# An earlier verdict, one piece for two chunks of y, and smaller clears, in a one-core gated-attention and feed-forward kernel

## The chip, the cores and the metric

The kernel runs on one core of a Trainium2 chip. The core has five engines that run side by side, each through its own queue in program order: TensorE (PE; its weight loads are listed as PEld), VectorE (DVE), ScalarE (ACT), GpSimd (POOL) and SyncE (SP), which issues most transfers. The metric is the device time of one execution in microseconds (us). A time is the median of several executions.

## The reference

Inputs are q, k, v, a_re and a_im of shape 4 batches x 8 heads x 768 steps x 48, and four weight matrices. Everything is float32 in the reference.

```
mag   = sqrt(a_re**2 + a_im**2);  scale = minimum(mag, 0.999) / (mag + 1e-6)
a     = (a_re + i a_im) * scale                # per step and per key element d
S[t]  = a[t, :, None] * S[t-1] + outer(k[t], v[t])       # complex 48 x 48 state per head
y[t]  = q[t] @ real(S[t])
x     = y as 3072 tokens x 384                 # the heads side by side
out   = ((x @ w1) * (x @ w2)) @ w3 @ w_out     # 384 -> 1024 -> 1024 -> 384
```

## The kernel before

The four batches are cut into eight units u = 0 to 7 of half a sequence each (384 steps, all 8 heads); u even begins a batch, u odd goes on from the state that the even one left. A unit has three chunks c of 128 steps.

**Stages.** At the head the weights are read, converted, and w3 @ w_out is formed once as `w3o` (lines 1025 to 1074: `row_load`, `row_work`, `fuse`). For each unit `gates(u)` turns the gates into running products of magnitude and sums of angle with logarithms, exponentials, scans and sines on ACT and DVE, multiplies them into q and k, and moves the results into the layouts `QL` and `KL`. The attention of a unit is made of four steps: `turn` (line 724) transposes k on TensorE (`tp`) and copies it out as `KT` (ACT, L733); `state` (line 787) forms the chunk's contribution `kv` to the state and adds it into one of three buffers `T`; `scores` (line 736) forms q k for half the heads (`sc`, L745) and evicts the lower triangle into one of two buffers `A` with a predicated copy on DVE (L748); `outputs` (line 760) forms y of one chunk out of A and V, and of QL and T (L779), and copies it to `xT` (ACT, L781). The feed-forward part of unit u-1 runs among the attention of unit u: eight `ab` steps (L820 twice three products, an ACT copy, a DVE multiply L826), then the sums `So` (L848), one row block with `w3o` (L909, `o`), and for the other two row blocks seven half-size products `p1` to `p7` (L873) whose sums are formed on DVE (L855). Beside all this, from 101.9 us on, POOL runs `check_weights` (line 972): it reads parts of the inputs again and counts which elements lie in the range that the fast path needs (`look`, `seen`).

**The order.** `pieces(u)` lists the attention of a unit as a list of short lists; `unit` puts between them the feed-forward steps of the unit before (`rest`), evenly by count, except that the last two of `rest` come at the end. `run` emits them in this order on TensorE, and books the gate steps, the looks and other work of ACT, DVE, POOL and SP with a clock of its own (line 1171 on) wherever they fit. So a change in `pieces` also moves some instructions of ACT and DVE. Every engine executes its own queue strictly in order.

**The verdict.** `judge(0)` compares the extremes that were collected from the gates, and `seen`, with their limits (seven small DVE instructions, L1090 and L1092), and `judge(1)` sums the counts over the partitions with one TensorE product (L1097) and writes the verdict `good` (L1101). At the very end every engine loads `good` (L1356) and branches on it (L1357): if it is 0, the whole computation is done again by `general`, for any inputs; otherwise the engines jump past that code to the closing barrier (L1391).

**Padding.** Heads are 48 wide and stand 64 apart in V and T. TensorE reads windows of 32 columns that reach into the 16 columns of padding, so these must be zero.

Of the kernel before, what the change touches and what calls it, by code (L numbers as in the profile page):

```python
# [375 lines left out]
def kernel(  # L376
# [36 lines left out]
    nc = tc.nc  # L413
    B, H, D, S = qt.shape
# [102 lines left out]
    def take_qk(u):  # L517
        g = g_t.setdefault(u, {})
        g["q"] = gate_pool[u % 2].tile([P, KD, TT], FP, tag="q", name="q")
        g["k"] = gate_pool[u % 2].tile([P, KD, TT + 1], FP, tag="k", name="k")  # L520
# [196 lines left out]
    def step(ops, n=1):  # L717

        for _ in range(n):
            for op in ops:  # L720
                if op is None or op == "move":
                    break

    def turn(u, c, x):

        src = L_t[u][2 + x]
        if x == 0:
            KT_t[u, c] = two.tile([P, H, DG, 2, KD], FP, tag="KT", name="KT")
        tp = ps_v.tile([P, KD, C], FP, tag="v", name="tp")
        for f in range(KD):  # L730
            nc.tensor.transpose(out=tp[:, f], in_=src[:, f, c * C:(c + 1) * C], identity=ident)  # L731
        with tc.high_priority():
            nc.scalar.copy(out=KT_t[u, c][:, :, :, x].rearrange("p h d f -> p f d h"),  # L733
                           in_=tp.rearrange("p f (d h) -> p f d h", h=H))

    def scores(u, c, x):
        QL, KL = L_t[u][0:2]
        w = slice(c * C, (c + 1) * C)
        A = Ab[(u * UC + c) % 2]
        n = H // 2  # L740
        sc = Sc[x]
        for s0 in SPANS:
            for j in range(n):
                g = (s0 // SB + j) % LANES
                nc.tensor.matmul(out=sc[SB * g:SB * g + SB, j, s0:C], lhsT=KL[:, x * n + j, w][:, s0:s0 + SB],  # L745
                                 rhs=QL[:, x * n + j, w][:, s0:C], start=True, stop=True)
        with tc.high_priority():
            masked[:] = [nc.vector.copy_predicated(out=A[:, x * n:(x + 1) * n], data=sc,  # L748
                                      mask=mask)]
# [32 lines left out]

    Tb = [singles.tile([2 * D, H, 64], FP, name=f"T{i}") for i in range(3)]
    for T in Tb:
        nc.gpsimd.memset(T, 0.0)

    def state(u, c):

        KT, V = KT_t.pop((u, c)), g_t[u]["vr"][:, c].rearrange("p (h d) -> p h d", d=D)
        n = u % 2 * UC + c  # L790
        T = T_t.get((u // 2, n))
        kv = ps_v.tile([2 * D, H, D], FP, tag="v", name="kv")
        for hd in range(H):
            rows = KT[:, hd].rearrange("p d x f -> p (d x f)")
            for g in range(0, 2 * D, SB):
                nc.tensor.matmul(out=kv[g:g + SB, hd], lhsT=rows[:, g:g + SB], rhs=V[:, hd], start=True, stop=True)  # L796
        Tn = Tb[(u * UC + c) % 3]
        with tc.high_priority():
            if T is None:
                nc.scalar.copy(out=Tn[:, :, 0:D], in_=kv)  # L800
            else:
                add = nc.vector.tensor_tensor(out=Tn[:, :, 0:D], in0=kv, in1=T[:, :, 0:D], op=OP.add)
                if (u, c) == (0, 1):

                    tc.add_manual_dep(add.ins, begun[-1].ins.name, ORDER, reason="begun")
        if c == UC - 1:
            rho = L_t[u][1][:, :, TT:TT + 1].to_broadcast([2 * D, H, D])
            nc.vector.tensor_tensor(out=Tn[:, :, 0:D], in0=Tn[:, :, 0:D], in1=rho, op=OP.mult)
        T_t[u // 2, n + 1] = Tn
        if u + 1 < NU and c == UC - 1 - u % 2:  # L810
            load_v(u + 1)
# [211 lines left out]
    def rounding():  # L1023

        stack = ExitStack()
        for n, k in (("raw", 2), ("low", 2)):
            cv[n] = stack.enter_context(tc.tile_pool(name=n, bufs=k))
        return stack
# [74 lines left out]
    for A in Ab:  # L1103
        nc.vector.memset(A, 0.0)
    for V in Vb:
        nc.gpsimd.memset(V, 0.0)

    def pieces(u):

        sc = [[("sc", lambda c=c, x=x: scores(u, c, x)) for x in range(2)] for c in range(UC)]  # L1110
        tr = [[("tr", lambda c=c, x=x: turn(u, c, x)) for x in range(2)] for c in range(UC)]
        kv = [("kv0" if u % 2 == c == 0 else "kv" if c < UC - 1 else "rho", lambda c=c: state(u, c)) for c in range(UC)]
        y = [("y" if u % 2 or c else "y0", lambda c=c: outputs(u, c)) for c in range(UC)]

        if u % 2:
            return [[("need", u), tr[0][0]], [tr[0][1]], [tr[1][0], kv[0]], [tr[1][1]], [kv[1]], sc[0], sc[1] + [y[0]],
                    sc[2] + [y[1]], [y[2], ("end", u)]]
        return [[("need", u), tr[0][0]], [tr[0][1]], [tr[1][0], kv[0]], [tr[1][1]], [tr[2][0], kv[1]], [tr[2][1]],
                [kv[2]] + sc[0], sc[1] + [y[0]], sc[2] + [y[1]], [y[2], ("end", u)]]

    def ffn(u, parts=1):
        ab = [("ab", lambda j=j: ffn_ab(u, j)) for j in range(KF)]
# [8 lines left out]
    def unit(u, rest, ahead):  # L1131

        seq = [("begin", u)] + rest[:ahead]
        rest = rest[ahead:]
        p = pieces(u) + [[]]
        n = len(p)
        first = [i * (len(rest) - 2) // (n - 1) for i in range(n)] + [len(rest)] if u > 1 else [0, 1, 2, 3, 3, 4, 4, 5, 5, 5, 6]
        for i in range(n):
            seq += rest[first[i]:first[i + 1]] + p[i]
        return seq  # L1140
# [137 lines left out]
    with tc.manual_schedule(engines={mybir.EngineType.PE}):  # L1278

        phase = rounding()  # L1280
        row_load(0, 4)
        load_gates(0)
        row_load(1, 2)
        row_load(2)
        row_load(3)
        take_qk(0)
        steps = gates(0, True)
        for f in range(KF):
            row_work(f)
            if f == 0:  # L1290
                load_qkv(0)
            if f + 4 < KF:
                row_load(f + 4)
            if f == VLOAD:
                load_v(0)
                turn_v(0)
            if f >= KF - 2:
                continue
            for j in range(KF):
                fuse(f, j)  # L1300
            step(steps, (3, 2, 2, 2, 1, 1)[f])
        work = w12_work()
        for _ in steps:
            pass
        for f in work[:2]:
            f()
        for f in range(KF - 2, KF):
            for j in range(KF // 2):
                fuse(f, j)
        fill = [lambda f=f, j=j: [fuse(f, j + x) for x in range(2)] for f in range(KF - 2, KF) for j in range(KF // 2, KF, 2)]  # L1310
        steps = gates(1, False)
        take_qk(1)
        rest = ffn(0, 2)
        work = work[2:]
        for i, p in enumerate(pieces(0)):
            for kind, f in p:
                if kind not in ("need", "end"):
                    f()
            if i in (1, 3, 6, 9):
                fill.pop(0)()  # L1320
            if i == 0:
                for f in work[:2]:
                    f()
                load_qkv(1)
                turn_v(1)
            step(steps, 5 if i == 0 else i >= 6)
            if i in (5, 7):
                work[2 + (i == 7)]()
        with tc.manual_schedule(engines={mybir.EngineType.Activation, mybir.EngineType.DVE, mybir.EngineType.Pool, mybir.EngineType.SP}):

            paced.append(True)
            work[4](False)

            def head(i):
                rest[i][1]()
                if i in (2, 3):
                    work[2 + i]()
                if i == 4:
                    phase.close()
                    late.append(fast.enter_context(tc.tile_pool(name="late", bufs=1)))  # L1340
                    late.append(fast.enter_context(tc.tile_pool(name="looks", bufs=1)))
                    looks.append(check_weights(late[1]))
                    streams.append((1, out_weights()))
            seq = [("abw" if i in (2, 3) else "ab", lambda i=i: head(i)) for i in range(HEAD)]
            for u in range(1, NU):
                seq += unit(u, rest[HEAD:] if u == 1 else ffn(u - 1), AHEAD[u])
            seq += ffn(NU - 1, 2)
            gate["ops"] = steps
            clock.update(POOL=0.0, SP=0.0, DMA=0.0)
            ready.clear()  # L1350
            ready.update(at=6.5, r2=6.3, k=7.7)
            advance()
            run(seq[:-6] + [("judge", 0)] + seq[-6:-2] + [("judge", 1)] + seq[-2:])
    fast.close()

    value = nc.values_load(good[0:1, 0:1], min_val=0, max_val=1)  # L1356
# [38 lines left out]
```

## Time and profile before

| | before |
|---|---|
| median of 3 executions | 562.1 us (561.05 to 562.63) |
| the profiled execution, its own time | 560.6 us |
| its span in the trace | 558.7 us |
| granted TensorE clock, mean | 0.985 |
| TensorE busy | 524.4 us, 94% |
| VectorE busy | 364.0 us, 65% |
| ScalarE busy | 274.8 us, 49% |
| GpSimd busy | 362.7 us, 65% |
| share of TensorE in the chain that ended last | 79% |

Times inside the trace are microseconds from the start of the span. The chain of work that ended last is followed back from the last instruction to whatever released it; an engine's busy time says little where it runs beside others. In tables of instructions a name ending in q (POOLq, SPq) is an engine's sequencer: it runs loads of registers, branches, semaphores and DRAINs, which are not counted as busy. Products in float32 appear as two matmul instructions each, so x8 in the chain stands for four products.

### The profile page before, as it was taken

Reading aid. Unit: us, or ns where it says so; the run is one execution under the profiler, and the core shown is the slowest. Engines: PE = TensorE matmul, PEld = TensorE weight load, DVE = VectorE, ACT = ScalarE, POOL = GpSimd, SP = SyncE. Lnnn points to the kernel's source line nnn. Section 1 sums busy time; section 2 is a strip of 40 time slices with the busy share of each in tenths; the row PEclk is TensorE's granted clock in tenths of the full one; section 3 lists DMA queues with packets and bytes.
Section 4 is the critical chain, followed back from the end, with each engine's and each line's share of the span. In section 5 each row is a group of like instructions: output and inputs, shape, how many; then the busy total and the mean of one; then the engine's idle time right before and its main releaser. Section 6 shows DMA issues by size and latency. Waiting matters only on the chain.

```text
span 558.7 us, 13227 instructions
## 1 busy us (share of the span) xinstructions
PE 524.4 (94%) x5474; PEld 358.8 (64%) x5474; DVE 364.0 (65%) x514; ACT 274.8 (49%) x389; POOL 362.7 (65%) x425
## 2 busy tenths in 40 slices
PE   4779889998999999999999999999999999999993
PEld 2345565566656785669666875687567856696572
DVE  7998399778685866687576756695848664421141
ACT  6988766585377325742475237722774242111100
POOL 3000000198888888888899889898998888886000
PEclk9899979999999999999999999999999999999998
DMA  8996978279559626892579245943595228322001
GB/s 260 354 406 166 285 210 279 65 167 196 137 125 242 182 106 174 204 265 77 145 192 222 83 118 152 241 130 102 136 234 156 64 69 212 77 70 70 0 2 49
DMA packets 73190, 89.73 MB, mean 161 GB/s; under 512 B 31776, under 2 KB 62944, under 8 KB 72352
## 3 DMA queue, kind: packets, MB, share of 16 engines
q1 hardware_dynamic: 67040, 69.78, 47.2%
q0 software_dynamic: 6080, 19.01, 11.6%
q8 instruction: 45, 0.74, 0.6%
q14 instruction: 25, 0.20, 0.1%
HBM read 65.14 MB, written 4.72 MB: 125 GB/s over the span
## 4 chain that ended last, share of the span: by engine, by line
PE 79%; DVE 8%; ACT 5%; issue 2%; DMA 2%; SPq 1%; DVEq 0%; ACTq 0%
PE m L820 45%; PE p L873 11%; PE y L779 7%; PE o L909 6%; PE sc L745 5%; DVE So L848 2%; PE kv L796 2%; DVE gA L624 2%; PE tp L731 2%; PE f L1070 1%; ACT gZ L576 1%; ACT low L955 1%; DMA im<-in_a_im_dram 1%; DMA k<-in_k_dram 1%; ACT gR L576 1%
## 5 line engine op out<-in xcount | busy, mean ns | idle before, releaser
L820 PE MATMUL m<-xT,w1s 128*128 128x384 f32 x384 | 135.0, 488 | 0.0
L820 PE MATMUL m<-xT,w2s 128*128 128x384 f32 x384 | 134.3, 486 | 0.0
L820 PEld LDWEIGHTS m<-xT,w2s 128*128 128x128 f32 x384 | 73.0, 190 | 50.9
L820 PEld LDWEIGHTS m<-xT,w1s 128*128 128x128 f32 x384 | 71.4, 190 | 44.9
L826 DVE TENSOR_TENSOR ab<-m,a 128x384 f32<-128x384 f32 x64 | 35.4, 553 | 91.4 <-PE m L820 83.1
L1016 POOL TENSOR_SCALAR look<-look 128x256 f32<-128x256 f32 (+1 forms) x84 | 88.4, 1053 | 7.3
L997 POOL TENSOR_TENSOR seen<-seen,look 128x256 bf16<-128x256 bf16 (+1 forms) x84 | 69.5, 828 | 6.8
L825 ACT COPY a<-m 128x384 f32<-128x384 f32 x64 | 30.3, 473 | 77.8 <-PE m L820 77.8
L981 POOL MEMSET seen<- 128x256 bf16 x1 | 0.3, 312 | 101.9 <-DVE w2s L965 101.9
L1013 POOL TENSOR_TENSOR look<-look 128x256 f32<-128x256 f32 (+1 forms) x72 | 59.5, 826 | 1.9
L909 PE MATMUL o<-w3o,ab 128*128 128x384 f32 x160 | 54.1, 487 | 0.0
L1015 POOL TENSOR_SCALAR look<-look 128x256 f32<-128x256 f32 (+1 forms) x44 | 50.4, 1146 | 5.1 <-DMA look<-in_a_re_dram 1.9
L781 ACT COPY xT<-y 128x384 f32<-128x384 f32 x24 | 11.4, 477 | 76.6 <-PE y L779 76.6
L992 POOL DMA_DIRECT2D look<-in_w_dram x56 | 33.6, 599 | 16.6 <-POOL seen L997 16.6
L733 ACT COPY KT<-tp 128x384 f32<-128x384 f32 x40 | 34.0, 856 | 18.1 <-PE tp L731 17.9
L1018 POOL TENSOR_TENSOR look<-look 128x256 f32<-128x256 f32 (+1 forms) x44 | 39.4, 896 | 3.7
L748 DVE COPY_PREDICATED A<-mask,sc 128x512 f32<-128x512 uint8 x48 | 33.0, 732 | 13.3 <-PE sc L745 12.8
L909 PEld LDWEIGHTS o<-w3o,ab 128*128 128x128 f32 x160 | 29.5, 190 | 18.3 <-issue 0.2
L779 PE MATMUL y<-A,V 128*32 128x128 f32 x768 | 40.2, 278 | 0.0
L1070 PE MATMUL f<-wo_s,w3s 128*128 128x384 f32 x96 | 37.2, 534 | 1.6 <-issue 1.6
L745 PE MATMUL sc<-QL,KL 96*32 96x32 f32 (+3 forms) x1536 | 33.5, 239 | 4.1 <-DVE A L748 1.9
L745 PEld LDWEIGHTS sc<-QL,KL 96*32 96x32 f32 x1536 | 29.2, 112 | 10.6 <-DVE A L748 4.4
(121 smaller groups left out, 904.7 us busy)
## 6 DMA issues: line engine op xcount, KB each, us to landing
look<-in_w_dram POOLq DMA_DIRECT2D x56, 256.0 KB, 3.5
raw<-in_w_dram SPq DMA_DIRECT2D x6, 1024.0 KB, 10.2
raw<-in_w_dram SPq DMA_DIRECT2D x8, 768.0 KB, 8.9
KL<-gR SPq DMA_DIRECT2D x24, 192.5 KB, 5.0
KL<-k SPq DMA_DIRECT2D x24, 192.5 KB, 5.6
re<-in_a_re_dram SPq DMA_DIRECT2D x24, 192.0 KB, 3.4
im<-in_a_im_dram SPq DMA_DIRECT2D x24, 192.0 KB, 3.3
k<-in_k_dram SPq DMA_DIRECT2D x24, 192.0 KB, 8.8
```

The costliest lines, as they stand in the source:

```text
L745: nc.tensor.matmul(out=sc[SB * g:SB * g + SB, j, s0:C], lhsT=KL[:, x * n + j, w][:, s0:s0 + SB], rhs=QL[:, x * n + j, w][:, s0:C], start=T ...
L779: nc.tensor.matmul(out=o, lhsT=a, rhs=b, start=s0, stop=s1)
L820: nc.tensor.matmul(out=m, lhsT=w[:, j * P // WB, f, j * P % WB:j * P % WB + P], rhs=xT_t[u][:, f], start=(f == 0), stop=(f == KD - 1))
L826: nc.vector.tensor_tensor(out=ab_t[u][:, j], in0=got[1], in1=a, op=OP.mult)
L873: nc.tensor.matmul(out=m[p], lhsT=a[:, f], rhs=b[:, f], start=(f == 0), stop=(f == KH - 1))
L909: nc.tensor.matmul(out=m, lhsT=ab_t[u][:, f, t * P:(t + 1) * P], rhs=w3o[:, f], start=(f == 0), stop=(f == KF - 1))
L997: nc.gpsimd.tensor_tensor(out=seen[:, 0:n], in0=seen[:, 0:n], in1=x, op=OP.add)
L1013: tt(out=x, in0=x, in1=x, op=OP.mult)
L1015: ts(out=y, in0=x, scalar1=high, scalar2=None, op0=OP.is_le)
L1016: ts(out=x, in0=x, scalar1=low, scalar2=None, op0=OP.is_ge)
L1018: tt(out=x, in0=x, in1=y, op=OP.mult)
L1070: nc.tensor.matmul(out=sums[j], lhsT=w3_t[f][:, j * P:(j + 1) * P], rhs=w3_t["wo"][:, f], start=(f == 0), stop=(f == KF - 1))
```

## The change

Three edits are made.

1. `judge(0)` is emitted twelve pieces from the end of the sequence instead of six, and `judge(1)` ten from the end instead of two. The end of the sequence is the feed-forward part of unit 7: eight `ab`, `spart`, and p1, p2, p4, p6, p7, o, p5, p3. So `judge(0)` moves from before p4 to before `ab` 5, and `judge(1)` from before p5 to before `ab` 7.
2. The y of chunks 1 and 2 stand in one piece, so a unit has one piece less, and the feed-forward steps are spread over one gap less. The lists for units 0 and 1 are adapted.
3. The clears of V and T touch only the columns 48 to 63 of each head.

In the emitted queues nothing changes on TensorE in units 0 and 1. In units 2, 4 and 6 p6 and p7 now stand together ahead of the third pair of scores, and the last two y follow each other. In units 3, 5 and 7 the last two y follow each other too, p6 and p7 stand together ahead of the third pair of scores, and the `o` product stands ahead of the last transpose of k, with p1 between that transpose and `kv`. On VectorE the sums of p7 come ahead of the third pair of evictions, and in units 3 and 5 the multiply of q (L636) comes ahead of the first pair. On ACT, in units 3 and 5, the copy `KT` comes behind the copy `ot` (L913) and the first of the two functions on `gR` comes behind the copy `U` (L878). On SP the load of `good` stands ahead of the last five output transfers. V's first transfer and T's first writes no longer wait for POOL.

```diff
@@ state buffers @@
     for T in Tb:
-        nc.gpsimd.memset(T, 0.0)
+        nc.gpsimd.memset(T[:, :, D:64], 0.0)
@@ value buffers @@
     for V in Vb:
-        nc.gpsimd.memset(V, 0.0)
+        nc.gpsimd.memset(V.rearrange("p c h e -> p (c h) e")[:, :, D:64], 0.0)
@@ pieces @@
         if u % 2:
             return [[("need", u), tr[0][0]], [tr[0][1]], [tr[1][0], kv[0]], [tr[1][1]], [kv[1]], sc[0], sc[1] + [y[0]],
-                    sc[2] + [y[1]], [y[2], ("end", u)]]
+                    sc[2] + [y[1], y[2], ("end", u)]]
         return [[("need", u), tr[0][0]], [tr[0][1]], [tr[1][0], kv[0]], [tr[1][1]], [tr[2][0], kv[1]], [tr[2][1]],
-                [kv[2]] + sc[0], sc[1] + [y[0]], sc[2] + [y[1]], [y[2], ("end", u)]]
+                [kv[2]] + sc[0], sc[1] + [y[0]], sc[2] + [y[1], y[2], ("end", u)]]
@@ unit @@
-        first = [i * (len(rest) - 2) // (n - 1) for i in range(n)] + [len(rest)] if u > 1 else [0, 1, 2, 3, 3, 4, 4, 5, 5, 5, 6]
+        first = [i * (len(rest) - 2) // (n - 1) for i in range(n)] + [len(rest)] if u > 1 else [0, 1, 2, 3, 3, 4, 4, 5, 5, 6]
@@ unit 0 @@
-            if i in (1, 3, 6, 9):
+            if i in (1, 3, 6, 8):
                 fill.pop(0)()
...
-            step(steps, 5 if i == 0 else i >= 6)
+            step(steps, 5 if i == 0 else (i >= 6) + (i == 8))
@@ the sequence @@
-            run(seq[:-6] + [("judge", 0)] + seq[-6:-2] + [("judge", 1)] + seq[-2:])
+            run(seq[:-12] + [("judge", 0)] + seq[-12:-10] + [("judge", 1)] + seq[-10:])
```

## The prediction

> **What bounds the kernel now.** First I read the page: its chain of work that ended last is 79% TensorE, and TensorE is busy 94% of the span. So an edit counts if it shortens TensorE's own queue, fills one of its gaps, or shortens the two ends of the span where TensorE is not at work.
>
> ```profile
> PE 79%; DVE 8%; ACT 5%; issue 2%; DMA 2%; SPq 1%; DVEq 0%; ACTq 0%
> ```
>
> Second, the end. TensorE's last product ends at 549.9 and VectorE's last sum at 550.3, but the span is 558.7, and no engine is busy in those last 8 us. The instructions of `good` (start times are the last column), of line 1357 (the branch and what follows it), and of line 1391 (the closing barrier) fill them:
>
> ```profile
> L1356 POOLq TENSOR_LOAD <-good x1: 502/502/502, 547.5 to 547.5; - x1
> ...
> L1357 SPq EVENT_SEMAPHORE  x8: 17/17/17, 553.9 to 554.5; - x8
> ...
> L1357 POOLq COMPARE_BRANCH  x1: 45/45/45, 548.1 to 548.1; - x1
> ...
> L1357 SPq COMPARE_BRANCH  x1: 45/45/45, 551.0 to 551.0; - x1
> ...
> L1357 POOLq EVENT_SEMAPHORE  x1: 17/17/17, 550.8 to 550.8; - x1
> ...
> L1391 POOLq EVENT_SEMAPHORE  x4: 17/17/17, 557.9 to 558.6; - x4
> L1391 POOLq DRAIN  x3: 40/107/6933, 550.9 to 558.4; - x3
> L1391 SPq DRAIN  x3: 7/7/13, 555.3 to 558.1; - x3
> ```
>
> To be seen: POOL, idle since its last look ended at 513.9, gets the verdict at 547.5, branches at 548.1, does its next instruction at 550.8, and then spends 6.93 us in a DRAIN from 550.9 to 557.85. Its barrier instruction follows at 557.9. SP, the last of the others (it issues the last output transfer), signs the barrier at 555.3. So POOL ends the kernel, 2.5 us behind SP, and POOL's time is set by `good` (written at 547.4 to 547.5) and by nothing else that the trace shows.
>
> Third, the chain in order of time over unit 2, an even unit; columns are start, length, what:
>
> ```profile
> 195.44 1.25 PE sc L745 x64
> 196.69 0.88 PE y L779 x32
> 197.56 1.50 PE p L873 x8
> 199.06 1.25 PE sc L745 x64
> 200.32 1.76 PE y L779 x64
> 202.07 1.50 PE p L873 x8
> 203.57 1.90 PE y L779 x64
> 205.47 2.80 PE p L873 x16
> ```
>
> TensorE runs here without a gap, so its order matters only by what each kind costs behind another: a product p costs 1.50 us alone behind y or sc, but two in a row 2.80; a y costs 1.76 behind sc and 1.90 behind p. Fourth, the timeline of VectorE and POOL at the head:
>
> ```profile
> 4.19 1.79 DVE L961 TENSOR_SCALAR w3s<-raw 128x256 int32<-128x256 int32 x1
> ...
> 8.98 0.29 DVE L961 TENSOR_SCALAR w3s<-raw 128x256 int32<-128x256 int32 x1 [0.64 <-DMA raw<-in_w_dram]
> ...
> 11.56 0.56 DVE L591 TENSOR_TENSOR im<-im,gR 128x384 f32<-128x384 f32 x1 [0.38 <-DMA im<-in_a_im_dram]
> ...
> 3.14 2.69 POOL L1106 MEMSET V<- 128x1536 f32 x2
> ```
>
> The same 128x256 operation takes 1.79 us while POOL clears V, and 0.29 us afterwards.
>
> **The verdict.** `judge(0)` goes from before product 4 to before `ab` 5 of the last unit, `judge(1)` from before product 5 to before `ab` 7. No instruction is added. VectorE's part (six tests with their accumulator reads and one compare) ran from 538.58 to 540.51, 1.9 us. Behind the `ab` multiply at 523.84 to 524.40 it runs to about 526.4; the next multiply is due at 527.7, since VectorE waits 3.31 us for TensorE between two of them: nothing on the path. Its first instruction waits for POOL's last look; that ended at 513.92, 10 us sooner. The count product on TensorE (0.12 us on the chain, 547.00 to 547.12) costs 0.12 us in either place, and finds its operand ready. VectorE writes `good` right behind multiply 6 (531.58 plus 0.56): about 532.5 instead of 547.5. SP's load of the verdict now stands ahead of the last five output transfers, but these start near 544 and lose nothing.
>
> POOL then branches at 533.1, is past it at 535.9 (the 2.7 us of the rows), and its DRAIN ends at 542.8 if it stays 6.93 us. Next late is SP: last transfer issued until 550.99, branch at 551.04, next instruction 553.93 (2.85 us), 20 semaphore instructions until 555.33. ACT signs at 550.7, PE at 552.3, VectorE at 553.8, all from work that does not move. So the barrier closes at 555.38 instead of 557.90: **2.5 us**. What the trace does not show is why this DRAIN takes 6.93 us. Bounds: 2.5 us gained if it is POOL's own (it may grow to 19 us before it matters), nothing if it waits for something at the end of the kernel. I take 2.5: the instruction names no semaphore, POOL's own transfers had all ended at 510, and nothing else ends at 557.85.
>
> The Trainium skill (VectorE: DVE Perf Modes, "The DRAIN you can't avoid") gives the closing DRAINs of all engines as about 12 ns, always the same. The rows of ACT, PE, VectorE and SP agree (7 to 17 ns), POOL's 6.93 us does not; taken strictly, the rule would make those 6.9 us a hidden wait for the rest of the kernel and this term 0.
>
> **y of two chunks in one piece.** The same TensorE instructions in another order, in units 2 to 7. An even unit now runs y0, p6 p7, sc, y1 y2, p5 p3. Before, by the rows from y0 on: 1.50 + 1.25 + 1.76 + 1.50 + 1.90 + 2.80 = 10.71. After: 2.80 + 1.25 + 1.76 + 1.76 + 2.80 = 10.37. Gain 0.34, three times: 1.02. In an odd unit (chain from 241.22) the o product also moves ahead of the last transpose, and p1 between that and kv. Before: 0.33 + 5.16 + 0.81 + 1.50 + 1.26 + 1.50 + 1.25 + 1.76 + 1.50 + 1.25 + 1.76 + 2.80 + 1.90 + 2.80 = 25.58. After: 5.16 + 0.33 + 1.30 (p behind a transpose, as at 189.47) + 0.88 (kv behind p, as at 191.72) + 1.50 + 1.25 + 1.50 + 1.25 + 1.76 + 2.80 + 1.25 + 1.76 + 1.76 + 2.80 = 25.30. Gain 0.28, three times: 0.84. Together 1.86.
>
> Covers, unit by unit. (a) y2 now follows y1 at once and needs the third pair of score evictions on VectorE. In unit 2 the last product before the scores ends at 200.36, its two sums at 201.1, the pair (1.37 us) at about 202.5, and y1 at 203.37: 0.85 us in hand. (b) In odd units kv waits for ACT's copy KT, which now has only p1 beside it: transpose done at 246.87 by the row's lag, copy of 0.88 us from 246.95 to 247.83, kv due at 248.0: 0.2 us in hand, against 5.16 us before. (c) In units 3 and 5 the multiply q (L636, 1.43 us) now stands ahead of the first evictions on VectorE: it runs 250.9 to 252.3, the pair to 253.6, and the second score group wants those banks at 253.1 and 253.8: 0 to 0.2 us each. Its load of q landed at 249.5, 1.4 us sooner (unit 5: 367.0 against 369.5). The gaps before kv at 190.8, 309.5 and 428.5 (0.94, 1.22, 0.81 us) come from VectorE's sums and scans ahead of ACT's KT, which do not move; they stay. Bounds for this edit: 2.1 gained (nothing waits, and transitions cost a little less than the rows), 0.6 lost (covers (b) and (c) miss by 0.5 us each, in five places); I take 1.7, the sum less 0.15 for (c), since every cover computes as holding.
>
> **The clearing.** POOL's five memsets took 1.44 + 2.69 = 4.13 us. By their rows (0.48 us for 512 elements, 1.35 for 1536: 0.85 ns an element) the strided ones of 128 and 384 take 3 x 0.16 + 2 x 0.37 = 1.2 us, 4.1 us at most if strides cost as much as full rows. POOL has nothing else until 101.9, so only VectorE's 1.79 us operation can gain: up to 1.5. But VectorE then waits longer for the raw weights at 8.98 and for the transfer of im at 11.56, which nothing here makes earlier: 0. If it is wrong, up to 1.5 gained, or 0.5 lost when weight loads that SP can issue 0.6 us sooner slow the landing of im.
>
> The Trainium skill (SBUF — State Buffer, "Who interferes with whom") says that GpSimd and some VectorE forms exclude each other for a whole instruction; the 1.79 against 0.29 fits, and by the rule alone the head would gain the full 1.5 and the time come to 556.4.
>
> **Sum.** 2.5 + 1.7 + 0 = 4.2 us: the profiled execution's 560.6 (span 558.7 and 1.9 around it) would be 556.4. The median of the runs shown, 562.1, is 1.5 above that execution; taken off it: **557.9 us**.
>
> **Rivals.** *POOL's DRAIN is not its own length.* For: 6.93 us against 0.04 to 0.17 for POOL's other DRAINs. Against: no semaphore, idle queues. Then only the order counts: 562.1 - 1.7 = 560.4. *The order gives nothing*, as small waits in (b) and (c) take it back; 562.1 - 2.5 = 559.6. *Slower: y2 waits for the third eviction pair.* For: that pair now queues behind two more sums, and VectorE's operations vary (1.33 to 1.69 us for L640). Against: 0.85 us in hand. Whatever it is late beyond that is paid in each of six units: it decides from 0.7 us beyond (6 x 0.7 = 4.2, all that is gained); a pair late by one more operation of VectorE, 1.7 us beyond, gives 562.1 + 6 x 1.7 - 4.2 = 568.1.
>
> **How the numbers follow.** Forecast 0.70, order gives nothing 0.10, DRAIN tied to the end 0.13, slower 0.07. A measurement of this kernel tells 0.3%, 1.7 us, from no change: below 560.4 is faster. Forecast and second rival are faster (0.80); the first rival lies at the edge and is put mostly to "same" (0.12), the rest of it and the third rival to slower (0.08). Range: the low end takes the two upper bounds, 557.9 - 1.5 (head) - 0.4 (order) = 556.0; the high end, 560.6, takes in both milder rivals.
>
> **What would show it.** After: `good` near 531, POOL's long DRAIN over before 545, SP the last to sign, 5.0 us from VectorE's last sum to SP's signature, 5.8 to the end. Chain: p in pairs behind y0, y 3.52 us for x128, units 2 to 7 shorter by 0.28 to 0.34 each. Head: L961 at 0.3 us, the first im multiply still near 11.5. Wrong if POOL's DRAIN again ends the span, if a gap stands before y2 or before kv in odd units, or if scores wait for evictions behind q.

## The result and the profile after

| | before | after | predicted |
|---|---|---|---|
| median of 20 executions each | 562.12 us (560.06 to 565.14) | 557.21 us (555.38 to 562.76) | 557.9 us (556.0 to 560.6) |
| ratio after / before, 95% interval | | 0.9917 (0.9900 to 0.9934) | |
| the profiled execution, its own time | 560.6 us | 557.56 us | 556.4 us |
| its span | 558.7 us | 555.6 us | 554.5 us |
| granted TensorE clock, mean | 0.985 | 0.987 | |

The kernel is faster by 4.9 us in the medians, where 4.2 were forecast. The two profiled executions differ by less, 3.0 us, and the prediction's steps can be checked only inside the traces. I cut each trace into the head (start to the first `ab` product, L820), the units 1 to 7 (from the first L820 of one feed-forward part to that of the next), and the closing (VectorE's last sum, L855, to the end of the span); the tail from unit 7 to that sum is 46.10 us in every one of them.

| us | head | unit 1 | units 2 to 7 | closing |
|---|---|---|---|---|
| before | 85.38 | 62.52 | 356.32 | 8.36 |
| after | 84.78 | 62.97 | 355.53 | 6.26 |
| difference | -0.60 | +0.45 | -0.79 | -2.10 |

First the closing, in the instructions of `good` (the load, then the branch L1357, then the barrier L1391; times are min, median and max in ns, then first and last start in us):

```profile
L1356 POOLq TENSOR_LOAD <-good x1: 497/497/497, 531.5 to 531.5; - x1
...
L1357 SPq EVENT_SEMAPHORE  x8: 17/17/17, 553.4 to 554.0; - x8
...
L1357 DVEq COMPARE_BRANCH  x1: 72/72/72, 549.7 to 549.7; - x1
...
L1357 SPq COMPARE_BRANCH  x1: 45/45/45, 549.8 to 549.8; - x1
...
L1391 POOLq DRAIN  x3: 40/107/6933, 534.7 to 555.4; - x3
L1391 SPq DRAIN  x3: 7/7/13, 554.8 to 555.1; - x3
```

POOL gets its verdict at 531.5, its DRAIN takes the same 6.933 us as before but from 534.7, so it is over at 541.7 under TensorE's work; POOL then stands at the barrier until 554.9. SP signs last, at 554.8, as forecast. But SP's next instruction comes 3.60 us after the end of its branch here, against 2.85 before.

Second, the chain of waits over unit 2 (start, length, what):

```profile
196.79 0.88 PE y L779 x32
197.66 2.80 PE p L873 x16
200.46 1.25 PE sc L745 x64
201.71 3.62 PE y L779 x119
205.34 2.80 PE p L873 x16
```

From y0 at 196.79 to 208.14 the pieces are 0.88, 2.80, 1.25, 3.62, 2.80: the order and the durations of the prediction, with 0.10 us more in the y pair (3.62 for 3.52). Units 3 and 5 in the same chain:

```profile
250.80 1.50 DVE q L636
252.30 0.67 DVE A L748
...
253.01 1.38 PE sc L745 x64
...
378.18 2.62 PE y L779 x91
380.79 0.36 issue
381.16 1.30 PE y L779 x34
```

In unit 3 the second score group stands behind the first eviction, and that behind q: cover (c), short by about 0.2 us. This is also why the page's chain now leaves TensorE for the load of q there, and reads

```profile
PE 65%; DMA 10%; DVE 10%; ACT 6%; SPq 5%; issue 3%; DVEq 0%; ACTq 0%
```

without TensorE being less of a bound: it is still busy 94% of the span. In unit 5 the y pair is torn by a gap of 0.36 us that has no releaser ("issue"), and costs 4.27 instead of 3.52. No step of the prediction speaks of such a gap.

Third, the head on VectorE:

```profile
4.18 0.23 DVE L961 TENSOR_SCALAR w3s<-raw 128x256 int32<-128x256 int32 x1
...
10.63 0.56 DVE L591 TENSOR_TENSOR im<-im,gR 128x384 f32<-128x384 f32 x1 [0.48 <-DMA im<-in_a_im_dram]
```

L961 fell from 1.79 to 0.23 us, and the multiply of im still waits for its transfer.

### The profile page after: what moved, and what is told of

Read it like the earlier page. It is cut to its first block, busy times and chain, and to the rows that moved or that the text cites. A ratio compares the mean times of both kernels' runs of the same rounds, so it can differ in the third digit from the quotient of the medians.

```text
span 555.6 us, 13216 instructions
## 1 busy us (share of the span) xinstructions
PE 521.1 (94%) x5474; PEld 359.6 (65%) x5474; DVE 361.1 (65%) x514; ACT 275.3 (50%) x389; POOL 355.5 (64%) x425
## 4 chain that ended last, share of the span: by engine, by line
PE 65%; DMA 10%; DVE 10%; ACT 6%; SPq 5%; issue 3%; DVEq 0%; ACTq 0%
PE m L820 36%; PE p L873 10%; PE y L779 6%; PE sc L745 5%; PE o L909 4%; DMA k<-in_k_dram 4%; DVE gA L624 2%; SPq L701 2%; DVE So L848 2%; DMA raw<-in_w_dram 2%; ACT low L955 2%; DMA q<-in_q_dram 2%; PE kv L796 1%; PE tp L731 1%; SPq L546 1%
## 5 line engine op out<-in xcount | busy, mean ns | idle before, releaser
L820 PE MATMUL m<-xT,w1s 128*128 128x384 f32 x384 | 135.1, 488 | 0.0
L820 PE MATMUL m<-xT,w2s 128*128 128x384 f32 x384 | 134.3, 486 | 0.0
L820 PEld LDWEIGHTS m<-xT,w2s 128*128 128x128 f32 x384 | 73.0, 190 | 50.9
L820 PEld LDWEIGHTS m<-xT,w1s 128*128 128x128 f32 x384 | 71.3, 190 | 44.7
L997 POOL TENSOR_TENSOR seen<-seen,look 128x256 bf16<-128x256 bf16 (+1 forms) x84 | 73.0, 869 | 6.8
L1013 POOL TENSOR_TENSOR look<-look 128x256 f32<-128x256 f32 (+1 forms) x72 | 52.1, 723 | 2.5 <-DMA look<-in_w_dram 0.6
L1018 POOL TENSOR_TENSOR look<-look 128x256 f32<-128x256 f32 (+1 forms) x44 | 39.2, 892 | 3.7
L1070 PE MATMUL f<-wo_s,w3s 128*128 128x384 f32 x96 | 35.8, 517 | 1.7 <-issue 1.7
## 6 DMA issues: line engine op xcount, KB each, us to landing
raw<-in_w_dram SPq DMA_DIRECT2D x6, 1024.0 KB, 10.2
```

The lines of the kernel that those rows point to most:

```text
L820: nc.tensor.matmul(out=m, lhsT=w[:, j * P // WB, f, j * P % WB:j * P % WB + P], rhs=xT_t[u][:, f], start=(f == 0), stop=(f == KD - 1))
L997: nc.gpsimd.tensor_tensor(out=seen[:, 0:n], in0=seen[:, 0:n], in1=x, op=OP.add)
L1013: tt(out=x, in0=x, in1=x, op=OP.mult)
L1018: tt(out=x, in0=x, in1=y, op=OP.mult)
L1070: nc.tensor.matmul(out=sums[j], lhsT=w3_t[f][:, j * P:(j + 1) * P], rhs=w3_t["wo"][:, f], start=(f == 0), stop=(f == KF - 1))
```

## The experiments

Times are medians, with the kernel before on the same chip beside them; "profiled once" is a single execution, and the runs of one kernel spread by 3 to 8 us.

**The kernel before again (`e0_before`).** 

> The kernel before, unchanged, for a second trace: how far does one execution differ from another in each stage? Theory 'stages vary by themselves': the first ab product (85.38 in the first trace, 84.78 after the change) lies anywhere between 84.4 and 85.8, the transfer of im lands between 10.6 and 11.6, single units differ by up to 0.7 us through the gaps before kv and TensorE's gaps without a releaser. Rival 'the stages repeat, so the differences between the two traces are the change': each of these within 0.1 us of the first trace. POOL's long DRAIN: 6.93 us again, closing stretch (last sum of VectorE to the end of the span) 8.4 us under both.

Profiled once: 563.64 us, span 561.2. Head 85.62, unit 1 63.86, units 2 to 7 357.07, closing 8.52. So with nothing changed units 2 to 7 move by 0.75 us and unit 1 by 1.3 us from one execution to the next, and the heads of all traces below run from 83.8 to 86.4. Of the differences in the table above only the closing stands out by itself (8.36 and 8.52 against 6.26); the rest needs several traces.

**The verdict alone (`e1_verdict`).** The diff is the line of the sequence:

```diff
-            run(seq[:-6] + [("judge", 0)] + seq[-6:-2] + [("judge", 1)] + seq[-2:])
+            run(seq[:-12] + [("judge", 0)] + seq[-12:-10] + [("judge", 1)] + seq[-10:])
```

> Only the verdict is earlier; order and clears as before. Theory 'POOL's DRAIN was the end': closing stretch 5.9 to 6.6 us instead of 8.4 (SP signs last; the spread is SP's branch, 2.9 or 3.6 us to its next instruction), TensorE's products end within 0.5 us of before, time 1.8 to 2.5 us lower, 559.6 to 560.3 against 562.1. Rival 'most of the gain comes from order and head': under 1 us lower. Second question: is SP's branch 3.6 us here too (then the early load of the verdict on SP costs 0.7 us), or 2.9 (then the 3.6 us of the changed kernel's trace are chance)?

559.97 against 562.69 us, ratio 0.9945 (0.9920 to 0.9970). The closing is 6.34 us. The instructions of the closing barrier:

```profile
L1391 POOLq DRAIN  x3: 40/107/6933, 538.1 to 558.7; - x3
L1391 SPq DRAIN  x3: 7/7/13, 558.1 to 558.4; - x3
```

As in the kernel after, the long DRAIN moves forward with the verdict (538.1) and keeps its length, and SP is last; its next instruction comes 3.67 us after its branch here too. So this edit alone brings 2.0 us in the trace. The profiled span of 559.0 hides it, since unit 4 took 62.63 us in it instead of some 60.3; that is taken up below.

**The order alone (`e2_order`).** The edits of `pieces`, `first`, `fill` and `step` on top of before, that is, the change without the two clears and without the line of the sequence. 

> Only y of the last two chunks in one piece; verdict and clears as before. Theory of the prediction: units 2 to 7 together 1.7 us shorter, time 560.4 against 562.1. Theory after the trace of the changed kernel: each y pair costs 3.52 us and the products behind y0 2.80 (0.3 us less in each unit), but in odd units part comes back, as evictions behind q (0.1 to 0.2 us) and as a wait of TensorE with no releaser inside the double y (0.4 us in unit 5); sum 0.6 to 1.3 us shorter, time 560.8 to 561.5. Rival 'the order gives nothing': units 2 to 7 within 0.3 us of before.

560.80 us, ratio 0.9961 (0.9931 to 0.9991). The closing is that of before (8.34). Units 2 to 7 take 355.59 us. Over the traces of kernels whose TensorE stream is not padded (padding comes below; `e8_drain`, of 606 us, is left out):

| units 2 to 7, us | traces |
|---|---|
| old order | 356.32 (before), 357.07 (`e0_before`), 356.63 (`e3_clear`), 358.53 (`e1_verdict`) |
| new order | 355.53 (after), 355.59 (`e2_order`), 355.40 (`e6_store`) |

Every new one is below every old one. The means are 357.1 and 355.5; without `e1_verdict` and its disturbed unit 4 the first is 356.7. So the order is worth 1.2 to 1.6 us, at or above the upper end of the 0.6 to 1.3 expected after the first trace. Unit 5 is torn as in the kernel after:

```profile
378.70 2.62 PE y L779 x91
381.32 0.36 issue
381.68 1.30 PE y L779 x34
```

at the same instruction and of the same length (x91, then 0.36), though the early verdict and the small clears are absent: the gap comes with the order.

**The clears alone (`e3_clear`).** The two memsets. 

> Only the smaller clears. Theory of the prediction: L961 takes 0.2 to 0.3 us instead of 1.79, VectorE waits longer for the raw weights and for im, and the head (start to first ab product) does not change beyond what e0 shows as its own variation; time within 0.3 us of before. Rival 'the clear held the head': the raw weights and im land about 1 us earlier than before and the head is 0.6 to 1.5 us shorter, also compared with e0; time 561.0 to 561.5.

562.42 us, ratio 0.9993 (0.9969 to 1.0017). VectorE's timeline at the head, where L961 begins at 4.18 and takes 0.23 us as in the kernel after, goes on:

```profile
5.14 0.36 DVE L951 TENSOR_SCALAR low<-raw 128x384 int32<-128x384 int32 x1 [0.73 <-DMA raw<-in_w_out_dram]
...
7.09 0.29 DVE L961 TENSOR_SCALAR w3s<-raw 128x256 int32<-128x256 int32 x1 [0.99 <-DMA raw<-in_w_dram]
...
12.03 0.56 DVE L591 TENSOR_TENSOR im<-im,gR 128x384 f32<-128x384 f32 x1 [0.92 <-DMA im<-in_a_im_dram]
```

The 1.56 us that L961 loses come back as waits for transfers: 0.73, 0.99 and 0.26 for raw weights and 0.92 for im, 2.9 us together, where before they are 0.64 and 0.38, 1.0 together. The first im multiply starts anywhere from 10.2 to 12.0 us in the traces (10.6 to 11.6 with the old clears, 10.2 to 12.0 with the new), and the heads are 83.8 to 86.4 us. The clears move nothing that ends the head.

**TensorE's stream shifted (`e5_pad64`, `e5_pad128`).** To see whether the gap in unit 5 hangs on the place of the instructions in TensorE's stream, 16 small unused products (64 instructions with their weight loads), or 32, are put ahead of the kernel after's work at the head:

```diff
+    pad = ps_v.tile([P, TT], FP, tag="v", name="pad"); [nc.tensor.matmul(out=pad[0:SB, 0:SB], lhsT=ident[:, 0:SB], rhs=ident[:, 0:SB], start=True, stop=True) for i in range(16)]
```

> The changed kernel with 16 more small products (32x32 out of the identity, 64 instructions) early in TensorE's queue; nothing else. The output is the same. Theory 'TensorE's instructions arrive in blocks of 256, and a burst of small instructions can outrun the next block': every block boundary moves 64 instructions ahead in the bursts, so the gap without releaser in unit 5 (0.36 us between products of y2, unit 58.94 us) changes its place or goes, and units 3, 5 and 7 take other times among 58.2 and 59.0, while the head ends within its own variation. Rival 'the gap is a wait for data (the third evictions, QL or T)': unit 5 stays 58.94, units 3 and 7 stay 58.39 and 58.19.

> As e5_pad64 with 32 small products (128 instructions, half a block). Theory of blocks: again other places; between the two pads at least one leaves unit 5 at 58.2 without a gap. Rival 'wait for data': 58.39, 58.94 and 58.19 again.

Profiled once each: 552.92 and 555.28 us, with 562.26 for before. The gap in unit 5 is gone in both (58.19 us each). The chain of `e5_pad64` in unit 1, and then unit 5:

```profile
138.09 3.52 PE y L779 x128
...
374.38 3.52 PE y L779 x121
```

In unit 1 of the kernel after the chain has 1.26 us of issue at 134.52 and 0.92 at 138.86, among `sc`, and 0.86 at 143.18, in the y pair.

The same products run through in the one and are interrupted in the other. The table of transfers has a queue of its own for such a thing, q8 ("instruction"): 45 packets and 0.74 MB in the whole execution, so 16 KB each, and TensorE has by far the most instructions (5474 products and as many weight loads). For 378.0 to 380.5, just ahead of the gap in unit 5 of the kernel after, it shows

```profile
q8 instruction: 1, 0.02, 2.4%
```

that is one packet, for 0.96 us (2.4% of 16 engines over 2.5 us); it ran from 378.80 to 379.76, and the gap ended 1.4 us later, at 381.16. In the eleven traces other than that of `e8_drain` there are 30 gaps of over 0.1 us without a releaser among the small products `sc` and `y`, 0.13 to 2.02 us long (none of them in `e5_pad64`), and each ended 1.34 to 1.60 us after the end of such a packet.

The place of the gaps says the same. If TensorE's recorded instructions (products, weight loads and those of its sequencer) are counted in order of time, each of the 30 gaps stands at a count that is 193 or 194 beyond a multiple of 256: behind 1985, 2241 and 2498 instructions in unit 1 of before and after, behind 7874 in unit 5 of after and `e2_order`. So the gaps are waits for TensorE's next block of 256 instructions, in stretches where it gets through many short ones.

The old order has the same boundary, also within y2 of unit 5, and no gap there. In before a product p stands between y1 and y2, the 256 instructions ahead of the boundary take 5.69 us, and the packet has ended 3.8 us before TensorE gets there. In after y1 and y2 stand together, the 256 take 3.46 us besides the gap, and the packet ended 1.4 us before TensorE went on. So the new order makes a gap there possible, by putting short instructions closer together.

The Trainium skill (Runtime: NRT & Kernel Launch, "Instruction fetch mechanics") says that the stream is refilled in blocks of 16 KiB, and that crossing a block is mostly hidden. The packets of 16 KB agree with the first, and the count agrees with "mostly": of the 45 packets of the kernel after, 4 were followed by such a gap, all of them among the small products.

**Both leads together (`e9_best`), and the padding on before (`e10_before_pad64`).** `e9_best` is `e5_pad64` with the edit of `e6_store` below; `e10_before_pad64` is before with the 16 products. 

> The changed kernel with the 16 small products in TensorE's queue (e5_pad64) and the last two output transfers on ACT's queue (e6_store). Theory of blocks, and the closing of e6: unit 1 at 59.5 us instead of 63.0, units 3, 5 and 7 at 58.2 to 58.4, closing stretch 4.9 to 5.3; time 551.5 to 552.5 against 562.3, ratio 0.981 to 0.983. Rival 'the 552.9 of e5_pad64 was one lucky execution': time within 1 us of e6_store, 556 to 558.

> The kernel before with the same 16 small products and nothing else. If blocks of instructions decide, the kernel before gets the same 3 to 3.5 us in unit 1 (63.0 to 59.5; its queue there is the same as the changed kernel's), while its odd units stay at 58.5 or change by their own block boundaries: time 558.5 to 559.5 against 562.3. Rival 'the small products help only the changed order': within 1 us of 562.3.

`e9_best`: 556.21 us (554.22 to 557.63, 6 executions) against 561.72, ratio 0.9903 (0.9869 to 0.9936). `e10_before_pad64`: 560.24, ratio 0.9968 (0.9943 to 0.9994). Neither met the gain that was expected. What the ratio of `e10_before_pad64` gives, 1.8 us, is not located: its one trace, of 562.74 us, is slower than its median. The single 552.92 of `e5_pad64` lies below all six executions of `e9_best`, so as far as these runs tell it was a lucky one. With the same padding unit 1 took 59.49 us in `e5_pad64` and 60.84 in `e9_best`, where the chain has 0.26 us of issue at 138.21 and 0.64 at 141.56. The 63.31 us of unit 1 in `e10_before_pad64` have another cause: only 0.15 us of it is such a gap, but TensorE waited 2.10 us there for the transfer of k (128.67 to 130.77), and then the granted clock was 0.50 from 131.80 to 135.21, so that an `o` which costs 2.78 elsewhere took 4.26:

```profile
132.26 4.26 PE o L909 x8
```

The place of a block's end decides where a gap can be; whether and how long it is differs between executions: behind 1985 instructions it is 0.41 us in the trace of before and 1.94 in that of the same kernel in `e0_before`. Unit 5 took 58.19 in all three kernels that are the one after with padding, against 58.94 in after and `e2_order`, so that gap can be taken away. But the padding opens another: behind 4801 instructions, in unit 3, `e9_best` has a gap of 0.22 us (unit 3 59.01 instead of 58.39) and `e10_before_pad64` one of 0.37 (59.30 instead of 58.53), and no kernel without padding has one there. The whole of `e9_best` can't be told from after (0.9917) by these runs, nor from `e6_store` (0.9907), which has no padding.

**SP freed from the last transfers (`e6_store`).** The output transfers of unit 7's second halves are issued by ACT:

```diff
-            nc.sync.dma_start(out=out[r0:r0 + P, s], in_=o[t][:, s])
+            (nc.scalar if u == NU - 1 and half else nc.sync).dma_start(out=out[r0:r0 + P, s], in_=o[t][:, s])
```

> The changed kernel with the last two output transfers issued by ACT's queue instead of SP's. Theory 'SP's and VectorE's branches, 0.1 us apart, slow each other's way to the next instruction (3.6 to 3.8 us, against 2.9 and 3.1 where they were 0.4 to 0.6 us apart)': SP now branches some 2 us earlier and is past it in 2.6 to 3.0 us; ACT takes SP's place beside VectorE; VectorE signs last, 4.2 us behind its last sum, and the closing stretch is 4.9 to 5.1 us instead of 6.3: time 1.2 to 1.4 us below the changed kernel. Rival 'the early load of the verdict slows SP's branch': SP needs 3.6 us again, still hidden. Rival 'the transfer's own end is next': the closing stretch stays above 6.

556.91 us, ratio 0.9907 (0.9879 to 0.9935); the closing is 5.30 us instead of 6.26. The branches and what follows them:

```profile
L1357 SPq EVENT_SEMAPHORE  x8: 17/17/17, 550.0 to 551.3; - x8
...
L1357 SPq COMPARE_BRANCH  x1: 45/45/45, 547.3 to 547.3; - x1
...
L1357 ACTq COMPARE_BRANCH  x1: 54/54/54, 550.4 to 550.4; - x1
...
L1357 ACTq EVENT_SEMAPHORE  x1: 17/17/17, 553.8 to 553.8; - x1
```

SP, which branches 2.4 us ahead of VectorE here, is past it in 2.61 us; in the kernel after, 0.1 us behind VectorE, it took 3.60. Now ACT is last, with 3.33 us from the end of its branch to its next instruction, having branched 0.7 us behind VectorE. VectorE, which was expected to sign last, is 0.4 us ahead of it. What is gained in the closing, 1.0 us for the 1.2 to 1.4 expected, is 0.2% of the time and less than the interval.

**POOL without transfers of its own (`e8_drain`).** The looks' reads are issued by SP's queue instead of POOL's, at both places in `check_weights`:

```diff
-                nc.gpsimd.dma_start(
+                nc.sync.dma_start(
...
```

> The changed kernel with the looks' transfers issued by SP instead of POOL, for POOL's long DRAIN alone: SP's queue gets 68 more transfers in order, so the time may be several us longer and says nothing. Theory 'the 6.93 us are POOL closing its own transfer queue': without transfers of its own the first closing DRAIN of POOL is under 0.2 us like the others. Rival 'POOL's first closing DRAIN always takes this long, or waits for something in the kernel': 6.93 us again, or another number above 1 us.

Profiled once: 606.18 us with the looks' reads among SP's other transfers; only the barrier is read from it. POOL's part of it, which is 40/107/6933 in the kernel after:

```profile
L1391 POOLq DRAIN  x3: 40/55/82, 583.9 to 604.1; - x3
```

So the 6.93 us come with POOL's own transfers, whether they ended long ago or not. The Trainium skill (VectorE: DVE Perf Modes, "The DRAIN you can't avoid") gives such DRAINs about 12 ns, constant on all engines. POOL's take 40 to 82 ns when it has issued no transfers, and the long one 6933 ns, some 580 times that figure, when it has; here the measurement decides.

## Why the prediction was right, point by point

**Closing: right in its mechanism, 0.4 us too large.** Forecast 2.5, measured 2.10 (2.02 in `e1_verdict`). That the DRAIN is POOL's own length and starts with the verdict is shown by after, `e1_verdict` and `e8_drain`; the rival of a DRAIN that waits for the end is refuted. The mis-sized term is SP's: "branch at 551.04, next instruction 553.93 (2.85 us)", taken over as it was, with SP's signature 5.0 us behind VectorE's last sum. It came 5.45 us behind. SP's last transfer took 0.33 us to issue instead of 0.64, so SP branched at 549.8, 0.1 us behind VectorE instead of 0.3 to 0.7 as in the traces with the late verdict, and both then waited longer for their next instruction: SP 3.60 against 2.85, VectorE 3.71 against 3.04 (all from the end of the branch). The prediction had ACT, PE and VectorE sign "all from work that does not move", and kept SP's figures too; the work did not move, but VectorE signed 0.7 us later behind its last sum, and PE, which now branches early, 1.5 us sooner. `e6_store` and `e9_best`, where SP branches alone, show 2.61 and 2.64 for SP, with the early load of the verdict present, so that load is not the cause. Whether two engines that branch at nearly the same time slow each other is not settled. For it speak the 3.47 to 3.67 us of SP in after, `e1_verdict` and `e8_drain`, 0.1 us behind VectorE; against it, that in the two padded kernels the branches were as close and SP took only 3.05 and 3.16, and that in the traces with the late verdict ACT, POOL and PE branch within 0.1 us of each other and ACT and POOL are past it in 2.4 to 2.8 us.

**Order: right in its mechanism, 0.1 to 0.5 us too large, with one cost missed.** The sum was 1.86, less 0.15 for cover (c): 1.7. Measured over several traces 1.2 to 1.6, in the pair of profiled executions 0.79. Part by part:

- Even units, forecast 0.34 each. Their gaps before `kv` vary by themselves (0.34 to 1.72 us over the traces), so I take them out: the three units then last 59.26, 59.26, 59.25 in before, and 58.95, 58.93, 58.93 in `e2_order`, 0.32 each. In after they last 59.06, 59.01 and 58.93, where the y pair took 3.62, 3.60 and 3.52.
- Odd units, forecast 0.28 each. Undisturbed they last 58.53 in the old order and 58.19 in the new: 0.34. The difference is that `kv` behind a p took 0.81 us (366.05 in after), where the sum had 0.88. Unit 7 is 58.52 to 58.53 in all traces of the old order and 58.19 in all of the new.
- Cover (c), 0 to 0.2 in units 3 and 5: 0.20 in unit 3 of after and of `e2_order` (58.39), none in `e6_store` (58.19). Within the bounds.
- Covers (a) and (b) held: no gap stands before y2 or before `kv` in odd units. The slower rival, y2 late for its evictions, did not occur.
- Not in the sum: the gap in unit 5's y pair, 0.75 us with what it slows (58.94 for 58.19), in after and `e2_order`; 58.43 in `e6_store`. It is a wait for a block of instructions, at a boundary that the old order crosses without one. The prediction had read from unit 2 that "TensorE runs here without a gap, so its order matters only by what each kind costs behind another", and did not ask whether the gaps of unit 1 in the trace of before (0.41, 0.92 and 0.59 us, without releaser) could appear in other units when small products stand closer together.

So the rival "the order gives nothing" would have seemed confirmed by odd units 3, 5 and 7 of the profiled execution alone (together 0.05 us faster instead of 0.84), and `e2_order`'s ratio of 0.9961, with an interval below 1, speaks against it.

**Clears: right.** Forecast 0, ratio 0.9993; the reason given, that VectorE then waits for raw weights and im, is what the waits of `e3_clear` show. The memsets took 0.48 for three and 0.77 for two in POOL's timeline of after, 1.25 us together for the estimate of 1.2. What POOL's clear costs VectorE is seen (1.79 to 0.23), and the 1.5 us that this would have given by itself are not there in the time.

**The sum.** By ratios the parts give 3.1 (`e1_verdict`), 2.2 (`e2_order`) and 0.4 us (`e3_clear`), each within 1.4 to 1.7; together 5.7, for 4.7 of the whole change, which agrees within these errors. In the traces the closing gives 2.1 and the order 1.2 to 1.6, so 3.3 to 3.7 of the 4.2 forecast are located. That the medians show 4.9 is within the interval of the ratio (3.7 to 5.6 us); whether anything more than chance adds to it stays open. The located parts are 0.5 to 0.9 us less than forecast and the gain of the medians 0.7 more, so that the median came this near is in part luck.

## What to carry to other kernels

Read the closing barrier engine by engine: an engine whose closing is long, here POOL with 6.93 us after transfers of its own, should get its last input early, and then the next engine must be costed anew, and not with the numbers that it had while the first one covered it. In a kernel of several thousand short TensorE instructions, sum a reordering from rows, but compare it over several traces and by the undisturbed units: a gap without a releaser can be a wait for the next block of instructions, and an edit that puts small products closer together, or shifts them in the stream, can open or close one. An operation that gets nearly eight times faster at the head is worth nothing where the transfer behind it lands no sooner.

## What the runs showed of the hardware

- TensorE waits for its own instructions: gaps of 0.13 to 2.02 us among small products, every 256 instructions or a multiple of that apart, ending 1.34 to 1.60 us after a 16 KB packet of the instruction queue. Most blocks pass without one.
- POOL's closing DRAIN is 6.933 us whenever POOL has issued transfers, even over 20 us after the last of them (all traces but `e8_drain`), and 0.04 to 0.08 us when it has issued none.
- From the end of the branch over the unused code to the next instruction POOL takes 2.5 to 2.8 us, ACT 2.4 to 3.3, SP 2.6 to 3.7 and VectorE 3.0 to 3.7. What makes the difference is open.
- A gap of TensorE of 1.69 to 1.72 us before `kv` in unit 4, in three traces (`e1_verdict`, `e5_pad128`, `e10_before_pad64`), was followed by half clock for 3.4 us, and so was the gap of 2.10 us in unit 1 of `e10_before_pad64`; gaps before `kv` of up to 1.33 us were not. The length of one gap doesn't decide it: gaps of 1.94, 2.02 and 2.10 us among the small products of unit 1 (`e0_before`, `e1_verdict`, `e2_order`) were not followed by half clock either. The windows of `e1_verdict` behind the gap before `kv` (309.64 to 311.35); columns are the window, its length, busy us and instructions of PE, PEld, DVE, ACT and POOL, the granted clock, the DMA share and GB/s:

```profile
312.00:314.00 2.00, 1.94 (x82) 1.79 (x72) 1.68 (x3) 0.26 (x1) 1.83 (x3) 0.71 0.25 31
314.00:316.00 2.00, 2.00 (x14) 1.88 (x7) 0.81 (x2) 0.00 (x0) 1.60 (x4) 0.50 0.82 283
```

and its chain there, where a `p` that costs 1.50 us elsewhere takes 2.53:

```profile
314.19 2.53 PE p L873 x8
```

That unit took 62.63 us instead of the 60.48 in before, which is nearly all of the 2.2 us by which units 2 to 7 of `e1_verdict` exceed those of before.
